# A fused attention and feed-forward kernel: the sums of probabilities times values go to any free PSUM bank instead of a fixed one, with the scheduling tables tuned anew

## The chip, the cores and the metric

One core of one Trainium2 chip. The metric is the device time of one execution in microseconds (us), as the median of several executions. A span is the time inside one profiled execution from its first to its last recorded instruction; in the profiled executions of this study it is 1.7 to 2.4 us shorter than the time. Engines are called PE (TensorE), ScalarE (ACT in the profile), VectorE (DVE), GpSimd (POOL) and SP (SyncE).

## The reference

```python
# x: 1 x 2048 x 640, bf16; H = 32 heads of Dh = 20; one K and one V head for all; F = 1536
xn = layernorm(x)
q = (xn @ wq) split into 32 heads;  k = xn @ wk;  v = xn @ wv
p = softmax(q @ k.T * Dh**-0.5)            # 32 x 2048 x 2048 probabilities
a = (p @ v) put together over heads @ wo
f = relu(xn @ w1 + b1)**2 @ w2 + b2
out = x + a + f
```

## The kernel before

The work on probabilities is cut into 2048 score tiles of 128 keys by 512 queries, each one PSUM bank. A tile's exponential is made on ScalarE (1480 tiles, two or three of them in one instruction, line 910) or approximated on VectorE and GpSimd in four terms (568 tiles). PE then adds probabilities times values ("PV") over the 16 key tiles of a block (four heads, 512 queries) in one bank, at four positions side by side. There are 32 blocks. At the end of each, VectorE copies the sum out (line 978, 30 times; the last two go another way).

The program that builds the kernel is a list scheduler: it settles the order of every engine's instructions when the kernel is built. Constants steer it, some of them in a table with an entry for each stretch of the run.

```python
NB = 7                       # banks 0..6: scores, projections, feed-forward
PVB = 7                      # bank 7: the PV sum, always
RULES = {3: {...}, 4: {...}, ...}      # steering constants by stretch  [cut]

def bank_state(bk):          # None: taken; otherwise the time from which it is free
    if bank_busy[bk]: return None
    o = bank_rel[bk]         # the instruction that empties it
    ...                                                       # [cut]

def make_act(st_):           # one exponential over n neighbouring banks
    ...
    deps = [st_["qk"]] + [pv_of[t[:2]] for t in st_["old"] if t is not None]
    return Op(..., [lambda e: e.activation(out=PT[:, s0:s0 + n, :], in_=ps[:, b0:...:db, :], func=AF.Exp, ...)], deps)

def make_pv(b, kt):          # PV of one key tile, four heads
    first, last = b not in pv_begun, pv_count[b] == KT - 1
    for h in range(HPG):
        parts.append(mm(ps[32 * h:32 * h + 32, PVB, :], vx[:, kt, :], PT[:, sl, :], first, last, (0, 32 * h)))
    if first and b > 0:
        deps.append(tn_op[b - 1])        # the copy of the block before
    ...                                                       # [cut]

# end of a block: the copy
tn = op(f"TN{b}", "DVE", 0.60, lambda e: e.tensor_copy(out=OR[:, a, :], in_=ps[:, PVB, :]), [lastpv] + or_users[a], prio=0)
```

The softmax here doesn't subtract the row's maximum and nothing guards it: scores larger than these inputs give would overflow.

## Time and profile before

The time was 705.52 us (median of 3; 704.88 to 706.26), the profiled span 703.64. The two views below were read only after the result, and they carry the explanation. The first gives the busy time of each engine by stretch of the span; the columns are the stretch, its length, then busy time and number of instructions of PE, PEld (weight loads), DVE, ACT, POOL, then clock and DMA.

```profile
0.00:40.00 40.00, 37.05 (x564) 17.29 (x565) 30.46 (x103) 31.57 (x45) 24.22 (x49) 1.00 0.48 143
40.00:694.00 654.00, 651.84 (x9062) 194.69 (x9058) 610.61 (x1013) 654.00 (x693) 401.36 (x217) 1.00 0.23 57
```

From 40 to 694 us ScalarE is busy for 654.00 of 654.00 us. The second view keeps ScalarE's groups of 45 to 694 us apart by shape; after the bar stand busy time, mean ns of one, and idle time before them.

```profile
L910 ACT ACTIVATE PT<-ps 128x1024 bf16<-128x1024 f32 x641 | 599.6, 1195 | 0.0
L910 ACT ACTIVATE PT<-ps 128x1536 bf16<-128x1536 f32 x47 | 74.6, 1617 | 0.0
```

No idle time at all. Everything before 40 us is in ScalarE's timeline (start, length, then in brackets the idle time before it):

```profile
15.30 12.46 ACT L910 ACTIVATE PT<-ps 128x1024 bf16<-128x1024 f32 x13 [1.05 <-PE ps L367]
28.15 1.94 ACT L910 ACTIVATE PT<-ps 128x1024 bf16<-128x1024 f32 x2 [0.39 <-PE ps L367]
32.44 12.88 ACT L910 ACTIVATE PT<-ps 128x1536 bf16<-128x1536 f32 x13 [2.35 <-PE ps L367]
```

After the first exponential there are two holes.

### The profile page before, as it was taken

The numbers are of one execution on the slowest core, as the hardware profiler recorded it, in microseconds if no ns is written. First come the engines' busy times: TensorE is split into PE (matmuls) and PEld (weight loads), VectorE is DVE, ScalarE is ACT, GpSimd is POOL, SyncE is SP. The second block draws the span as 40 slices with busy tenths as digits, with TensorE's granted clock in tenths as the row PEclk, the third lists the DMA queues.
The fourth block names the chain that finished last, engine by engine and source line by source line (L and its number), as shares of the span: only waits on it lengthen the run. The fifth ranks groups of instructions, "written<-read, shape, count | busy, mean of one in ns | idle before, by whom it ended". The sixth has DMA issues, their size and how long they took to land.

```text
span 703.6 us, 22608 instructions
## 1 busy us (share of the span) xinstructions
PE 695.0 (99%) x9780; PEld 216.0 (31%) x9781; DVE 645.9 (92%) x1125; ACT 687.5 (98%) x739; POOL 427.3 (61%) x268
## 2 busy tenths in 40 slices
PE   8999999999999999999999999999999999999997
PEld 4422223233322223332322222323333222233333
DVE  7789999999999998989998998899899999999894
ACT  6899999999999999999999999999999999999995
POOL 4767556567566764666568765766665675644253
PEclk9999999999999999999999999999999999999999
DMA  6325422233337701211101001111112100031201
GB/s 201 98 70 153 115 78 58 81 97 80 84 85 160 162 20 25 55 40 37 52 18 40 23 22 28 29 47 26 46 42 51 36 22 23 20 106 51 55 26 39
DMA packets 42016, 44.00 MB, mean 63 GB/s; under 512 B 15540, under 2 KB 32772, under 8 KB 41788
## 3 DMA queue, kind: packets, MB, share of 16 engines
q1 hardware_dynamic: 39132, 36.93, 19.2%
q0 software_dynamic: 2208, 5.25, 3.9%
q8 instruction: 76, 1.25, 0.7%
q10 hardware_dynamic: 576, 0.38, 0.2%
q14 instruction: 24, 0.20, 0.1%
HBM read 28.03 MB, written 14.91 MB: 61 GB/s over the span
## 4 chain that ended last, share of the span: by engine, by line
ACT 95%; PE 4%; DMA 1%; DVE 0%; SPq 0%; issue 0%; DVEq 0%
ACT PT L910 94%; PE ps L367 3%; DMA x_sb<-in_A_x_dram 1%; PE ps L540 1%; ACT xnT L477 0%; ACT OC L421 0%; DVE out_sb L1164 0%; PE ps L568 0%; SPq L384 0%; ACT OC L422 0%; SPq L391 0%; PE ps L510 0%; PE ps L496 0%; DVEq L227 0%; DVE PT L1164 0%
## 5 line engine op out<-in xcount | busy, mean ns | idle before, releaser
L910 ACT ACTIVATE PT<-ps 128x1024 bf16<-128x1024 f32 (+1 forms) x715 | 677.1, 1219 | 3.8 <-PE ps L367 3.8
L1083 DVE TENSOR_SCALAR tmore<-ps 128x512 uint16<-128x512 f32 x568 | 367.4, 683 | 31.7 <-PE ps L367 28.2
L1101 POOL TENSOR_SCALAR tmore<-tmore 128x2048 uint16<-128x2048 uint16 x109 | 206.4, 1900 | 171.1 <-PE ps L367 62.3
L367 PE MATMUL ps<-qT,kT 20*128 20x512 bf16 x2048 | 281.7, 384 | 1.9 <-ACT PT L910 0.8
L1101 POOL TENSOR_SCALAR x_sb<-tmore 128x2048 uint16<-128x2048 uint16 x100 | 189.3, 1902 | 79.4 <-DVE x_sb L1101 24.2
L367 PEld LDWEIGHTS ps<-qT,kT 20*128 20x128 bf16 x2048 | 71.6, 91 | 280.4 <-ACT PT L910 233.1
L367 PE MATMUL ps<-PT,vx 128*32 128x512 bf16 x1480 | 136.9, 386 | 0.2 <-ACT PT L910 0.2
L1101 DVE TENSOR_SCALAR x_sb<-tmore 128x2048 uint16<-128x2048 uint16 x135 | 96.1, 745 | 0.1
L367 PE MATMUL ps<-x_sb,vxs 128*32 128x512 bf16 x940 | 83.2, 382 | 0.0
L367 PE MATMUL ps<-xnT,w_sb 128*32 128x512 bf16 x960 | 77.2, 384 | 0.1
L367 PE MATMUL ps<-w_sb,big 128*32 128x320 bf16 x1536 | 74.5, 302 | 0.0
L367 PE MATMUL ps<-tmore,vxs 128*32 128x512 bf16 x764 | 69.6, 382 | 0.0
L1101 DVE TENSOR_SCALAR tmore<-tmore 128x2048 uint16<-128x2048 uint16 x82 | 61.5, 770 | 0.1
L367 PE MATMUL ps<-tmore,vx 128*32 128x512 bf16 x568 | 55.7, 382 | 0.0
L367 PEld LDWEIGHTS ps<-PT,vx 128*32 128x32 bf16 x1480 | 34.9, 94 | 62.1 <-issue 53.6
L367 PEld LDWEIGHTS ps<-w_sb,big 128*32 128x32 bf16 x1536 | 32.1, 95 | 29.3 <-issue 22.2
L648 DVE TENSOR_SCALAR hT_tmp<-ps,b1col 128x512 bf16<-128x512 f32 x48 | 35.8, 746 | 3.4 <-PE ps L367 2.7
L367 PE MATMUL ps<-xnT,wq_sb 128*32 128x512 bf16 (+1 forms) x480 | 33.7, 356 | 0.2 <-DVE tmore L1083 0.2
L367 PE MATMUL ps<-wo_c,OC 128*32 128x320 bf16 x608 | 30.9, 301 | 0.0
L367 PEld LDWEIGHTS ps<-x_sb,vxs 128*32 128x32 bf16 x940 | 21.3, 95 | 19.9 <-issue 13.4
L367 PEld LDWEIGHTS ps<-xnT,w_sb 128*32 128x32 bf16 x960 | 17.6, 94 | 26.7 <-issue 22.4
L367 PEld LDWEIGHTS ps<-tmore,vxs 128*32 128x32 bf16 x764 | 18.1, 95 | 16.4 <-issue 11.5
(81 smaller groups left out, 259.4 us busy)
## 6 DMA issues: line engine op xcount, KB each, us to landing
xbd<-b2d SPq DMA_DIRECT2D x16, 320.0 KB, 4.4
xbd<-in_A_x_dram POOLq DMA_DIRECT2D x8, 640.0 KB, 5.8
xr<-xbd SPq DMA_DIRECT2D x32, 160.0 KB, 2.4
w_sb<-in_B_w_dram SPq DMA_DIRECT2D x8, 480.0 KB, 4.4
big<-OR SPq DMA_DIRECT2D x71, 40.0 KB
big<-drs SPq DMA_DIRECT2D x71, 40.0 KB
out_dram<-out_sb SPq DMA_DIRECT2D x15, 160.0 KB, 1.8
qT<-QCr SPq DMA_DIRECT2D x108, 20.0 KB
```

The costliest lines, as they stand in the source:

```text
L367: return lambda e: e.matmul(out_, l, r, start=start, stop=stop, tile_position=tp)
L540: return [(lambda e, dt=dt: e.transpose(out=psbf(bk)[:, dt * 128:(dt + 1) * 128], in_=xn_sb[:, st, dt:D:DT], identity=ident[:])) for dt in ...
L648: o = Op(f"RL{qc}_{f}", "DVE", 0.66, [lambda e: e.tensor_scalar(out=hT_tmp[:, k % 2, :], in0=ps[:, bk, :], scalar1=b1col[:, f:f + 1], scal ...
L910: return Op(f"ACT{st_['j']}", "ACT", 0.05 + 0.4267 * n, [lambda e: e.activation(out=PT[:, s0:s0 + n, :], in_=ps[:, b0:b0 + (n - 1) * db + ...
L1083: d1 = op(f"D1_{n}_{i}", "DVE", 0.60, lambda e: e.tensor_scalar(out=L[:, cs].bitcast(U16), in0=ps[:, bank, :], scalar1=XA, scalar2=XB, op0 ...
L1101: p = op(f"P{j}_{n}", eng, 0.60 if eng == "DVE" else 1.86, lambda e, T=T, j=j, two=two: e.tensor_scalar(out=T.bitcast(U16), in0=L.bitcast( ...
```

## The change

The intent: while VectorE copies a block's sum out of the one PV bank, the next block's PV products cannot begin. If the next block may open any free bank, they need not wait.

```diff
-NB = 7
-PVB = 7
+NB = 8
+PV0 = 7
+pv_bank = {0: PV0}
+def bank_for(b):                      # the bank that is free first
+    if b in pv_bank: return pv_bank[b]
+    can = [(bank_state(bk), -bk) for bk in range(NB) if bank_state(bk) is not None and ...]
+    return -min(can)[1] if can else None
+def kept():                           # no score product takes that bank before the block has begun
+    b = pv_blk[0]
+    return bank_for(b) if b < NBLK and b not in pv_begun else None
 # make_pv, make_dpv
-        parts.append(mm(ps[32 * h:32 * h + 32, PVB, :], ...))
-    if first and b > 0:
-        deps.append(tn_op[b - 1])
+        parts.append(mm(ps[32 * h:32 * h + 32, bank, :], ...))
+    if first:
+        deps.append(bank_rel[bank])
 # the copy at a block's end
-    tn = op(..., e.tensor_copy(out=OR[:, a, :], in_=ps[:, PVB, :]), ...)
+    tn = op(..., e.tensor_copy(out=OR[:, a, :], in_=ps[:, pb, :]), ...)
+    tn.frees = pb
 # every table was tuned anew with it
-RULES = {3: {'PVA': 2.1, ...}, ...}                     # [cut]
+RULES = {2: {'ND': 1, ...}, ...}                        # [cut]
-PRIO = {'NM15': 2.12, 'NM10': 2.88, 'PW2': 0.96}
-NBEF = {'AG4': 10.21, 'NM7': 11.5, 'Qe0_1': 10.11, 'PW12': 25.33}
-QEACT = (0, 1, 2, 3)
-ACTST = (2, 5, 6)
+PRIO = {'XN1': 0.13}                                    # the start's order
+NBEF = {'S4a': 6.0, 'AG5': 10.23, 'PW1': 4.94}
+QEACT = (0, 1)
+ACTST = (0, 2, 4)
```

So the change has three parts that can be taken apart: the free bank, the table of rules, and the constants of the start. The cut parts also hold one further limit on VectorE's score products and two more constants of the start.

More of the change, by code (lines that the diff above doesn't have):

```diff
@@ L80 @@
 KEEP = 1
-RULES = {3: {'PVA': 2.1, 'PVD': 2.1, 'R3': 1, 'PP': 0.9},
-         4: {'PVA': 2.1, 'PVD': 2.1, 'R3': 1, 'PP': 0.9, 'WARM': 0.78},
-         5: {'D1P': 1, 'MPRIO': 0.5, 'PBIAS': 2.5},
-         6: {'D1P': 1, 'MPRIO': 0.5, 'PBIAS': 2.5, 'ND': 1, 'QKP': 0},
-         7: {'DQP': 2.05, 'URG': 2, 'PVD': 2.1, 'BEHIND': -0.3},
-         8: {'WARM': 0.85, 'DQP': 0.95},
-         10: {'ND': 1, 'NOPEN': 3},
-         11: {'ND': 1, 'NOPEN': 3},
-         12: {'EPS': 0.12},
-         13: {'EPS': 0.06, 'EVP': 0.3},
-         15: {'PBIAS': 0},
-         17: {'EPS': 0.06},
-         18: {'EPS': 0.12},
-         19: {'WARM': 0.78, 'PBIAS': 2.5, 'IDLE': 0.3},
-         21: {'PBIAS': 0, 'KEEP': 0},
-         23: {'EPS': 0.12},
-         25: {'R3': 1, 'EVP': 0.3},
-         26: {'R3': 1, 'EVP': 0.3, 'IDLE': 0.3, 'PVD': 2.1},
-         28: {'EPS': 0.12, 'URG': 3},
-         29: {'EPS': 0.12, 'URG': 3, 'KEEP': 3, 'EVP': 1.1, 'ND': 3},
-         31: {'PBIAS': 1, 'D1P': 1, 'PVD': 1.05},
-         32: {'PBIAS': 1, 'D1P': 1, 'PVD': 1.05, 'DGAP': 0.8, 'DQP': 0.95, 'SQP': 2, 'R3': 1},
-         36: {'PP': 0.9, 'BEHIND': -0.1, 'EVP': 0.3, 'PBIAS': 1.5},
-         37: {'URG': 3, 'JIT': 1.0, 'PVD': 1},
-         38: {'SQP': 0.7, 'URG': 3},
-         39: {'PP': 2.5},
-         40: {'PBIAS': 1},
-         41: {'PBIAS': 1, 'DGAP': 1.5, 'SQP': 0.7},
-         42: {'PBIAS': 1, 'DGAP': 1.5, 'SQP': 2, 'NOPEN': 3, 'ND': 2, 'PVD': 1},
-         43: {'PBIAS': 1, 'DGAP': 1.5, 'SQP': 2, 'NOPEN': 3, 'ND': 2, 'PVD': 1, 'R3': 9},
-         44: {'WARM': 0.78, 'KEEP': 3, 'DLAST': 7.5},
-         45: {'DGAP': 0.8, 'KEEP': 1, 'D1P': 3},
-         48: {'PBIAS': 1},
-         49: {'PBIAS': 1, 'R3': 1},
-         50: {'PBIAS': 1, 'R3': 1},
-         53: {'DLAST': 3.5},
-         54: {'DLAST': 3.5, 'EPS': 0, 'EVP': 0.3},
-         55: {'DLAST': 3.5, 'EPS': 0, 'EVP': 0.3, 'ND': 1},
-         56: {'EVP': 2, 'MPRIO': 1.0},
-         57: {'R3': 1, 'ND': 1},
-         58: {'BEHIND': -0.1, 'EPS': 0, 'PP': 4, 'R3': 1},
-         59: {'BEHIND': -0.1, 'EPS': 0, 'PP': 4, 'R3': 1, 'DRATE': 0.95, 'DLAST': 10, 'PVA': 2.1},
-         60: {'EVP': 1.1},
-         61: {'EVP': 1.1, 'SQP': 0.7},
-         62: {'EVP': 1.1, 'SQP': 0.7, 'KEEP': 3, 'R3': 1, 'NOPEN': 2, 'D1P': 3},
-         64: {'PP': 0.9, 'DRATE': 0.8},
-         65: {'R3': 1},
-         66: {'R3': 1},
-         67: {'EPS': 0.12, 'PVA': 1.05},
-         68: {'R3': 0},
-         69: {'R3': 0, 'JIT': 1.1}}
@@ new lines @@
+DJIT = 9.0
+RULES = {2: {'ND': 1, 'JIT': 1.1, 'PBIAS': 0.6},
+         3: {'DLAST': 5.5, 'NOPEN': 2, 'DJIT': 9, 'R3': 1},
+         4: {'DLAST': 5.5, 'NOPEN': 2, 'DJIT': 9, 'R3': 1, 'JIT': 0.75, 'DQP': 0.95},
+         5: {'DLAST': 5.5, 'NOPEN': 2, 'DJIT': 9, 'R3': 1, 'JIT': 0.75, 'DQP': 0.95, 'EPS': 0.12},
+         6: {'MPRIO': 0.9, 'PVD': 2.1, 'R3': 9},
+         10: {'DLAST': 7.5, 'PBIAS': 2.5, 'DGAP': 0.5},
+         11: {'DLAST': 7.5, 'PBIAS': 2.5, 'DGAP': 0.5},
+         12: {'DLAST': 5.5, 'PBIAS': 2.5, 'DGAP': 0.5, 'WARM': 0.78},
+         13: {'DLAST': 5.5, 'PBIAS': 1, 'DGAP': 0.5, 'WARM': 0.78, 'DRATE': 0.8},
+         14: {'NOPEN': 2, 'BEHIND': -0.1, 'MPRIO': 1.0},
+         15: {'IDLE': 0.5, 'NOPEN': 3, 'PVA': 1.05},
+         16: {'PP': 2.5, 'EVP': 0.5, 'PVA': 1.05, 'DGAP': 0.25},
+         17: {'DQP': 0.95, 'DJIT': 9, 'PBIAS': 1},
+         18: {'DQP': 0.95, 'DJIT': 9, 'PBIAS': 0.6, 'QKP': 0},
+         19: {'DLAST': 7.5, 'URG': 6, 'DJIT': 0.6},
+         20: {'DLAST': 6.5, 'URG': 6, 'DJIT': 0.6},
+         21: {'DLAST': 6.5, 'URG': 6, 'DJIT': 0.6, 'PVA': 1.05, 'PP': 2.5},
+         22: {'PVA': 1.05, 'JIT': 0.82},
+         23: {'PVA': 1.05, 'JIT': 0.82, 'PBIAS': 2.5, 'QKP': 0},
+         24: {'PBIAS': 2.5, 'PP': 4, 'DQP': 0.95, 'WARM': 0.72},
+         25: {'PBIAS': 2.5, 'PP': 4, 'DQP': 0.95, 'WARM': 0.72, 'MPRIO': 0.5, 'D1P': 0.5, 'DGAP': 1.5},
+         27: {'PBIAS': 2.5},
+         29: {'SQP': 2, 'URG': 2, 'PP': 2.5},
+         30: {'JIT': 0.82, 'DJIT': 0.6, 'DGAP': 1.5, 'DLAST': 2.5},
+         31: {'IDLE': 0.3, 'ND': 1, 'QKP': 0},
+         32: {'PBIAS': 0, 'JIT': 1.0},
+         33: {'JIT': 0.82, 'MPRIO': 0.9, 'PP': 2.5},
+         34: {'JIT': 0.82, 'MPRIO': 0.9, 'PP': 2.5, 'QKP': 0, 'DQP': 0.95},
+         38: {'ND': 3, 'URG': 3, 'PBIAS': 0.3, 'D1P': 0.5},
+         39: {'JIT': 0.75},
+         41: {'R3': 0},
+         42: {'SQP': 1.5, 'NOPEN': 1},
+         44: {'QKP': 0, 'R3': 1, 'BEHIND': 0.12, 'KEEP': 2},
+         45: {'QKP': 0, 'R3': 1, 'BEHIND': 0.12, 'KEEP': 3},
+         46: {'QKP': 0, 'R3': 1, 'BEHIND': 0.12, 'KEEP': 0},
+         47: {'QKP': 0, 'R3': 1, 'BEHIND': 0.12, 'KEEP': 0, 'DRATE': 1.1, 'ND': 3},
+         48: {'QKP': 0, 'R3': 1, 'BEHIND': 0.12, 'KEEP': 0, 'DRATE': 1.1, 'ND': 3},
+         49: {'QKP': 0, 'DRATE': 0.8, 'DLAST': 4.5, 'JIT': 0.75},
+         50: {'QKP': 0, 'DRATE': 0.95, 'DLAST': 4.5, 'JIT': 0.75, 'EVP': 2, 'PBIAS': 2.5},
+         51: {'QKP': 0, 'DRATE': 0.95, 'DLAST': 4.5, 'JIT': 0.75, 'EVP': 2, 'PBIAS': 2.5, 'D1P': 3, 'EPS': 0.12, 'DQP': 0.95, 'IDLE': 0.2},
+         53: {'KEEP': 3},
+         54: {'KEEP': 1, 'NOPEN': 1},
+         55: {'PP': 2.5},
+         56: {'PP': 2.5},
+         57: {'PP': 2.5, 'PVD': 0.95},
+         58: {'QKP': 0, 'URG': 6},
+         59: {'QKP': 0, 'URG': 6, 'JIT': 1.0, 'R3': 0, 'DRATE': 0.8},
+         60: {'QKP': 0, 'URG': 3, 'JIT': 1.0, 'R3': 0, 'DRATE': 0.8, 'BEHIND': 0.25, 'WARM': 0.78, 'EVP': 0.5},
+         61: {'QKP': 0, 'URG': 3, 'JIT': 1.0, 'R3': 1, 'DRATE': 0.8, 'BEHIND': 0.25, 'WARM': 0.78, 'EVP': 0.5, 'ND': 3},
+         62: {'DJIT': 0.6, 'JIT': 0.75},
+         63: {'DJIT': 0.6, 'JIT': 0.75, 'R3': 0},
+         64: {'DJIT': 0.6, 'JIT': 0.75, 'R3': 0, 'EPS': 0.06, 'PBIAS': 1.5, 'D1P': 1, 'WARM': 0.72},
+         65: {'DJIT': 0.6, 'JIT': 0.82, 'R3': 0, 'EPS': 0.06, 'PBIAS': 1.5, 'D1P': 3, 'WARM': 0.72, 'DQP': 0.95, 'SQP': 2},
+         66: {'DJIT': 9, 'JIT': 0.82, 'R3': 0, 'EPS': 0.06, 'PBIAS': 1.5, 'D1P': 3, 'WARM': 0.72, 'DQP': 0.95, 'SQP': 2},
+         67: {'DQP': 3, 'R3': 1},
+         68: {'DQP': 3, 'R3': 1, 'DGAP': 0.25, 'ND': 1, 'SQP': 2, 'PP': 4},
+         69: {'DQP': 3, 'R3': 1, 'DGAP': 0.25, 'ND': 1, 'SQP': 2, 'PP': 4}}
@@ L143 @@
 EARLYK = "F"
-FFN0 = 0.3
+FFN0 = 0.6
 OUT0 = 0.5
@@ L148 @@
 QCPOS = 0
-ACTST = (2, 5, 6)
-POOLXN = (2, 7, 9, 10, 11, 13, 14, 15)
+ACTST = (0, 2, 4)
+POOLXN = (7, 9, 10, 11, 13, 14, 15)
 ROWP = (-0.5, 0.6, 0.8, 1.2)
@@ L159 @@
 DEFAULTS = dict(EVP=EVP, PBIAS=PBIAS, MPRIO=MPRIO, DGAP=DGAP, DLAST=DLAST, DRATE=DRATE, BEHIND=BEHIND, IDLE=IDLE, URG=URG, NOPEN=NOPEN,
-                EPS=0.03, JIT=JIT, R3=R3, STATIC=STATIC, PVA=1, PVD=1, D1P=1, PP=4, SQP=2, DQP=3, QKP=0, ND=2, WARM=WARM, KEEP=KEEP)
+                EPS=0.03, JIT=JIT, R3=R3, STATIC=STATIC, PVA=1, PVD=1, D1P=1, PP=4, SQP=2, DQP=3, QKP=0, ND=2, WARM=WARM, KEEP=KEEP, DJIT=DJIT)
 class Ctr:
@@ L506, in fill_parts @@
         def fill_parts():
-            return [mm(ps[32 * jj:32 * jj + 32, PVB, :], zeros32[:, :], kT[:, 0:512], False, False, (0, 32 * jj)) for jj in range(4)]
+            return [mm(ps[32 * jj:32 * jj + 32, pv_bank[pv_blk[0]], :], zeros32[:, :], kT[:, 0:512], False, False, (0, 32 * jj)) for jj in range(4)]
         def warm_parts():
-            return [lambda e: e.matmul(ps[:, PVB, :], ones_bf[:, :], hT_tmp[:, 0, :], start=True, stop=True)]
+            return [lambda e: e.matmul(ps[:, PV0, :], ones_bf[:, :], hT_tmp[:, 0, :], start=True, stop=True)]
         def need_te(sts):
@@ L857, in make_step @@
             t0 = max(free["PE"], horizon() - par("JIT"))
-            st_of = {bk: bank_state(bk) for bk in range(NB)}
+            keep = kept()
+            st_of = {bk: bank_state(bk) if bk != keep else None for bk in range(NB)}
             ok = [bk for bk in range(NB) if st_of[bk] is not None and st_of[bk] <= t0 + 0.02]
@@ L920, in after_act, with pv_begin @@
                     pv_ready[key[0]].append(("A", key[1]))
+        pv_bank = {0: PV0}
+        bank_busy[PV0] = True
+        def bank_for(b):
+            if b in pv_bank:
+                return pv_bank[b]
+            can = [(bank_state(bk), -bk) for bk in range(NB) if bank_state(bk) is not None and not (par("STATIC") and bk in HELD)]
+            return -min(can)[1] if can else None
+        def kept():
+            b = pv_blk[0]
+            return bank_for(b) if b < NBLK and b not in pv_begun else None
+        def pv_begin(b):
+            if b not in pv_begun:
+                pv_bank[b] = bank_for(b)
+                bank_busy[pv_bank[b]] = True
+                pv_begun.add(b)
         def make_pv(b, kt):
@@ L924, in make_pv @@
             parts, deps = [], []
+            bank = bank_for(b)
             for h in range(HPG):
@@ L927, in make_pv @@
                 deps.append(o)
-                parts.append(mm(ps[32 * h:32 * h + 32, PVB, :], vx[:, kt, :], PT[:, sl, :], first, last, (0, 32 * h)))
+                parts.append(mm(ps[32 * h:32 * h + 32, bank, :], vx[:, kt, :], PT[:, sl, :], first, last, (0, 32 * h)))
             deps.append(v_op[kt // 4])
-            if first and b > 0:
-                deps.append(tn_op[b - 1])
+            if first:
+                deps.append(bank_rel[bank])
             return Op(f"PV{b}_{kt}", "PE", 0.222, parts, deps)
@@ L939, in make_dpv @@
             parts = []
+            bank = bank_for(b)
             for h in range(HPG):
                 i = s["order"].index(h)
-                parts.append(mm(ps[32 * h:32 * h + 32, PVB, :], wgt[:, kt, :], src[:, i * 512:(i + 1) * 512], first, last, (0, 32 * h)))
+                parts.append(mm(ps[32 * h:32 * h + 32, bank, :], wgt[:, kt, :], src[:, i * 512:(i + 1) * 512], first, last, (0, 32 * h)))
             deps.append(v_op[kt // 4])
@@ L945, in make_dpv @@
                 deps.append(vs_op[kt // 4][term - 1])
-            if first and b > 0:
-                deps.append(tn_op[b - 1])
+            if first:
+                deps.append(bank_rel[bank])
             return Op(f"DPV{b}_{kt}_{term}", "PE", 0.2205, parts, deps)
@@ L966, in emit_norm @@
             a = b % NOR
+            pb = pv_bank[b]
             if b >= NBLK - 2:
                 Tn, T2 = OR[:, a, :], QCr[:, 0, :]
-                tn = op(f"TN{b}", "DVE", 0.63, lambda e: e.transpose(out=Tn, in_=ps[:, PVB, :]), [lastpv] + or_users[a], prio=0)
+                tn = op(f"TN{b}", "DVE", 0.63, lambda e: e.transpose(out=Tn, in_=ps[:, pb, :]), [lastpv] + or_users[a], prio=0)
+                tn.frees = pb
                 rc = op(f"RC{b}", "DVE", 0.155, lambda e: e.reciprocal(out=Tn[:, DH:512:32], in_=Tn[:, DH:512:32]), [tn], prio=0)
@@ L977, in emit_norm @@
                 return
-            tn = op(f"TN{b}", "DVE", 0.60, lambda e: e.tensor_copy(out=OR[:, a, :], in_=ps[:, PVB, :]), [lastpv] + or_users[a], prio=0)
+            tn = op(f"TN{b}", "DVE", 0.60, lambda e: e.tensor_copy(out=OR[:, a, :], in_=ps[:, pb, :]), [lastpv] + or_users[a], prio=0)
+            tn.frees = pb
             tn_op[b] = tn
@@ L1041, in pool_banks @@
         def pool_banks():
+            keep = kept()
             if par("STATIC"):
-                return [bk for bk in POOLED if bk not in HELD and bank_state(bk) is not None]
-            fb = [bk for bk in POOLED if bank_state(bk) is not None]
+                return [bk for bk in POOLED if bk not in HELD and bk != keep and bank_state(bk) is not None]
+            fb = [bk for bk in POOLED if bk != keep and bank_state(bk) is not None]
             return fb if len(fb) > par("KEEP") else []
@@ L1055, in make_dqk @@
             if not fb or (len(fb) == 1 and behind()):
+                return None
+            if max(free["DVE"], free["PE"]) + sum(o.dur for o in dve_q if o.frees is not None) > free["PE"] + 0.43 + par("DJIT"):
                 return None
@@ L1119, in tail_bank @@
             bs = [bk for bk in range(NB) if (bk not in HELD or done) and bank_state(bk) is not None]
-            if tn_op.get(NBLK - 1) is not None and tn_op[NBLK - 1].fin is not None and not bank_busy[PVB]:
-                bank_rel[PVB] = bank_rel[PVB] or tn_op[NBLK - 1]
-                bs.append(PVB)
             return min(bs, key=lambda bk: (bank_state(bk), bk)) if bs else None
@@ L1229, in bass_parallel_sum__grouped_kv_mqa__dense_activation_squared_relu__prompt_kernel @@
             b = pv_blk[0]
-            if b < NBLK and (b == 0 or b - 1 in tn_op):
+            if b < NBLK and (b == 0 or b - 1 in tn_op) and bank_for(b) is not None:
                 for k, (kind, x) in enumerate(pv_ready[b]):
@@ L1324, in bass_parallel_sum__grouped_kv_mqa__dense_activation_squared_relu__prompt_kernel @@
             elif kind == "pv":
-                pv_begun.add(ap[1])
+                pv_begin(ap[1])
                 pv_of[(ap[1], pv_ready[ap[1]].pop(ap[2])[1])] = o
@@ L1328, in bass_parallel_sum__grouped_kv_mqa__dense_activation_squared_relu__prompt_kernel @@
             elif kind == "dpv":
-                pv_begun.add(ap[1])
+                pv_begin(ap[1])
                 s_, term = ap[3], ap[4]
```

## The prediction

> **What bounds the kernel now.** I read the page first, then the ScalarE groups kept apart by shape, the waits, the view of the line that evacuates the PV sums, and the timeline at one block's end.
>
> ```profile
> PE 695.0 (99%) x9780; PEld 216.0 (31%) x9781; DVE 645.9 (92%) x1125; ACT 687.5 (98%) x739; POOL 427.3 (61%) x268
> ...
> ACT 95%; PE 4%; DMA 1%; DVE 0%; SPq 0%; issue 0%; DVEq 0%
> ACT PT L910 94%; PE ps L367 3%; DMA x_sb<-in_A_x_dram 1%; PE ps L540 1%; ACT xnT L477 0%; ACT OC L421 0%; DVE out_sb L1164 0%; PE ps L568 0%; SPq L384 0%; ACT OC L422 0%; SPq L391 0%; PE ps L510 0%; PE ps L496 0%; DVEq L227 0%; DVE PT L1164 0%
> ```
>
> PE and ACT are both full, but a busy PE is not a PE at its peak; the chain that ended last settles it. 94% of the span lies on line 910, the exponential on ScalarE. In the chain in order of time it is one piece from 32.44 to 694.23 us.
>
> ```profile
> L910 ACT ACTIVATE PT<-ps 128x1024 bf16<-128x1024 f32 x665 | 621.9, 1190 | 1.4 <-PE ps L367 1.4
> L910 ACT ACTIVATE PT<-ps 128x1536 bf16<-128x1536 f32 x50 | 79.0, 1609 | 2.3 <-PE ps L367 2.3
> ```
>
> The work comes in 665 pairs and 50 triples of 512-column score tiles (1480 tiles; VectorE does the other 568 of 2048). Idle before them is 3.7 us in all. The mean of one (1190 ns) is longer than its turn, since neighbours overlap. From the start times of all 715 in the trace, the usual (median and 5th percentile) distance from a pair to the next start is 0.904 us; the shortest distances after a triple are 1.330 us.
>
> So the time can be taken apart:
> - first exponential starts at 15.30 us;
> - 714 full-speed turns: 664 x 0.904 + 50 x 1.330 = 666.76;
> - from first to last start there are 678.60 us, so 11.84 us are turns that came late: 3.20 before 40 us and 8.64 over the rest;
> - the last one lasts 1.25, and the tail after it 703.64 - 695.14 = 8.50;
> - time less span is 705.52 - 703.64 = 1.88.
>
> Only the start, the 8.64 and the tail can move unless tiles move between engines.
>
> Does PE wait for the evacuation of the PV sums, line 978?
>
> ```profile
> L978 DVE COPY OR<-ps x30: 674/681/692, 49.3 to 655.0; 128x512 f32<-128x512 f32 x30
> its engine sat idle before it (us, times) until:
>   PE ps L367: 0.3, 1
> who waited for it (us, times):
> busy tenths in 40 slices 0000000000000000000000000000000000000000
> ```
>
> The list under "who waited for it" is empty: no engine was seen idle for this copy. The kernel's instruction order was settled when it was built, and it puts other work there. At the block end whose copy runs from 299.99:
>
> ```profile
> 299.47 0.39 PE L367 MATMUL ps<-PT,vx 128*32 128x512 bf16 x4
> 299.83 0.39 PE L367 MATMUL ps<-qT,kT 20*128 20x512 bf16 x2
> 300.15 0.59 PE L367 MATMUL ps<-w_sb,big 128*32 128x320 bf16 x12
> ...
> 304.48 0.39 PE L367 MATMUL ps<-qT,kT 20*128 20x512 bf16 x2
> 304.80 0.40 PE L367 MATMUL ps<-PT,vx 128*32 128x512 bf16 x4
> ```
>
> PV stops at 299.86 and resumes at 304.80, with scores and feed-forward products in between and PE busy for 4.99 of the 5.00 us. Over the 30 copies the last PV of one block to the first of the next takes 1.57 to 4.94 us, median 2.2. The copy needs about 0.14 + 0.68 of that; the rest is choice of order. Nor are the late turns at those places: after 50 us they total 0.0135 us per us, and 0.014 and 0.006 us per us in the 2 us before and after a copy's start.
>
> **What the Trainium skill says.** "Perfetto Trace Analysis", section Matmuls: independent groups should rotate through PSUM banks so that evacuation of one overlaps the next group's products. That is the intent here, but the trace shows the overlap already had by other means. The same page, section Optimization Strategy, says that repeating bubbles on the engine that should be full can mean too little buffer. Here they are small: 480 of the 691 turns after 40 us are within 5 ns of the fastest, and the largest delay is under 0.3 us. "ScalarE: Activation LUTs", section "Step-by-step: what each stage is for", gives 0.833 ns per element whatever the function. The trace agrees: (1.330 - 0.904) / 512 = 0.832 ns. So the turns themselves cannot shrink.
>
> **The change part by part.**
> 1. The bank. The fixed PV bank goes; scores, projections and PV draw from eight. While a block is summing, seven are left, as before. At a block end the next PV may open another bank, so the pause can fall from a median of 2.2 us toward nothing. But while the next block has not begun, the best free bank is kept back for it, so scores gain little. What this saves in PE idle is zero by the view above. It lets the order be better balanced; of 8.64 us of late turns I give it 1, an estimate.
> 2. The split of work. Built, both programs have 2048 score products, 568 VectorE tiles, 3752 PV products and the same feed-forward products. ScalarE gets 657 pairs, 55 triples, 1 single: still 1480 tiles. Turns: 657 x 0.904 + 55 x 1.330 = 667.08, and the last single lasts about 1.19 - 0.43 = 0.76, together 667.84 against 666.76 + 1.25 = 668.01. Worth 0.2 us.
> 3. VectorE and GpSimd. Of the passes that derive further terms, 11 move to GpSimd (217 to 206 on DVE, 209 to 220 on POOL). That frees 11 x about 0.75 = 8 us of a VectorE that is 92% busy and not the bound, and adds 11 x 1.9 = 21 to a GpSimd at 61%. Neither is on the chain. PE gets 5 more warm-up products and 4 more zero products, under 3 us of filler in its waits.
> 4. The start, retuned along with it. ScalarE takes the statistics of row tiles 0, 2, 4 in place of 2, 5, 6 and hands two query evacuations (0.28 each) to VectorE; the order of normalizing and transposing changes. Two effects:
>    - First exponential. Now VectorE does statistics of a later tile from 7.88 and normalizes an early one only at 9.96; in the new order the early tiles come sooner. I estimate 0.5 to 1.5 us earlier, say 1.0.
>    - Third group of keys. The first 32 score tiles need only the first two groups, then ScalarE stands still, 30.09 to 32.44, for the third: VectorE copies two query evacuations (0.69 each, at 25.15 and 27.10) and only then normalizes a tile at 28.16 that the group needs. In the new order only one such copy lies ahead, and the second projection's 20 products (about 1.1 us of PE) come after the group. This could take most of the 2.35 us away, but an earlier first exponential also makes it ask earlier. For the 3.20 us of late turns I put 1.7.
>
>    Together about 2.5 us.
> 5. The tail. The last products are interleaved otherwise: after the final transpose 64 output products remain in place of 56. 8 x 0.034 us (16 took 0.54) is 0.3 worse; the shorter last exponential has been counted.
>
> Sum: -1.0 (late turns) - 0.2 (turns) - 2.5 (start) + 0.3 (tail) = -3.4 us, so 705.5 - 3.4 = 702.1; I say 702.
>
> **The rivals.**
> - Nothing comes of it: PV was never seen waiting, ScalarE's tiles are unchanged, and the start only shifts its waiting from one place to another. 705, plus or minus 1. For it speak the empty list and the keys gate; against it the 2.35 us hole with two avoidable copies ahead of it.
> - The late turns vanish: the 8.64 us come from PE being tied, and free banks loosen it. Best case 705.5 - 8.6 - 3.2 - 1.5 = 692, 1.9% faster, so not even this passes 2%. Against it: late turns do not gather at block ends.
> - A new wait: a score product meets a bank that VectorE has not emptied, or a GpSimd pass (1.9 us against 0.75) arrives late for its PV because 11 more were handed there. VectorE's busy share speaks for the first, GpSimd's 61% against the second. Doubling the late turns costs about 8 us: 711 at worst with a gain at the start.
>
> **Range and chances.** Spread comes from the start (-4 to +1) and the late turns (-4 to +3), not independent of how well the order suits the chip: 698 to 706. Past 2% needs under 691.4 or over 719.6; the first needs more than all the waste listed, the second more than twice today's late turns. Chances: faster 0.03, within 2% 0.95, slower 0.02.
>
> **What would show it.** Pair and triple turns should stay 0.904 and 1.330; late turns after 40 us should be 6 to 10 us; the hole near 32 us should be under 1.5; the first exponential should lie between 13.5 and 15.3; the tail should be 8.3 to 9.2; the pause between blocks' PV should shrink with PE no busier. I am wrong if the pause shrinks and the late turns fall to a third (the bank was what tied PE), or if they grow (the order no longer fits the chip).

## The result and the profile after

The changed kernel is correct and takes 706.59 us (median of 4; 706.53 to 707.07), against 705.81 (704.88 to 706.26) for the kernel before, timed with it. The ratio is 1.0014, 95% interval 0.9997 to 1.0032: the same. Here and below a ratio is the mean time of one kernel's fast runs over that of the other's fast runs of the same rounds, so not quite the ratio of the medians quoted. All runs were fast, except one of pin_new, which is left out.

The page after: the busy times, then the chain that ended last by engine.

```profile
PE 695.3 (99%) x9790; PEld 217.7 (31%) x9790; DVE 643.3 (91%) x1117; ACT 687.8 (98%) x735; POOL 446.5 (63%) x278
...
ACT 61%; PE 37%; DVE 1%; DMA 1%; issue 0%; POOL 0%; ACTq 0%; DVEq 0%
```

VectorE lost 2.6 us of work and GpSimd gained 19; PE and ScalarE stand as before. The chain now runs through PE for 37% of the span, where it had been 4%. That looks like a new bound and is not one. The chain is followed back from the end and steps onto PE where an exponential had to wait for it, then stays there: from such a wait at 639.53 us it runs back on PE to 444.17. One real wait, however small, sends it there for a long way. ScalarE's groups from 45 to 694 us, and the stretches, say how small:

```profile
L918 ACT ACTIVATE PT<-ps 128x1024 bf16<-128x1024 f32 x636 | 595.1, 1187 | 0.6 <-PE ps L374 0.3
L918 ACT ACTIVATE PT<-ps 128x1536 bf16<-128x1536 f32 x49 | 78.1, 1614 | 0.0
```

```profile
40.00:694.00 654.00, 651.70 (x9065) 195.66 (x9057) 609.86 (x1006) 653.42 (x690) 422.39 (x230) 1.00 0.23 57
```

ScalarE is idle for 0.6 us in 654. The pause that the change was made for did go: from the end of the last PV product of one block to the start of the first of the next it was 2.2 us (median of 30 blocks; mean 2.77), and is now 0.03 us in the mean and 0.49 at most. In 17 of the 30 blocks there is none at all: the first product starts before the modelled end of the last. PE got no less idle by it: from 40 to 694 us it is busy for 651.84 us before and 651.70 after. The pause had been full of other products all along.

**The start.** ScalarE's timeline after the change:

```profile
14.88 7.44 ACT L918 ACTIVATE PT<-ps 128x1024 bf16<-128x1024 f32 x8 [1.97 <-PE ps L374]
23.22 7.13 ACT L918 ACTIVATE PT<-ps 128x1024 bf16<-128x1024 f32 x6 [0.91 <-PE ps L374]
31.01 7.74 ACT L918 ACTIVATE PT<-ps 128x1536 bf16<-128x1536 f32 x7 [0.66 <-PE ps L374]
39.73 6.03 ACT L918 ACTIVATE PT<-ps 128x1536 bf16<-128x1536 f32 x6 [0.98 <-PE ps L374]
```

The hole of 2.35 us near 32 us has become three holes of 0.91, 0.66 and 0.98. Each ends 0.6 to 1.1 us after the keys of another group of four key tiles have been written by VectorE, and it begins where ScalarE had used up the groups that it had: 16 score tiles (of 16 per group) were done before the first, and 31 and 47 before the others, whose exponentials cover three tiles and so reach into the next group. Here are those writes, groups two, three and four, first before and then after the change:

```profile
19.35 0.75 DVE L554 TENSOR_SCALAR kT<-ps,nk 128x512 bf16<-128x512 f32 x1
30.94 0.75 DVE L554 TENSOR_SCALAR kT<-ps,nk 128x512 bf16<-128x512 f32 x1 [1.58 <-PE ps L367]
35.13 0.75 DVE L554 TENSOR_SCALAR kT<-ps,nk 128x512 bf16<-128x512 f32 x1 [1.80 <-PE ps L367]
```

```profile
21.36 0.75 DVE L561 TENSOR_SCALAR kT<-ps,nk 128x512 bf16<-128x512 f32 x1
29.67 0.75 DVE L561 TENSOR_SCALAR kT<-ps,nk 128x512 bf16<-128x512 f32 x1
38.16 0.75 DVE L561 TENSOR_SCALAR kT<-ps,nk 128x512 bf16<-128x512 f32 x1 [1.80 <-PE ps L374]
```

The third group comes 1.27 us sooner, the second 2.0 and the fourth 3.0 us later.

**Reading ScalarE by its ends.** The prediction took the span apart by the starts of the exponentials. Taken apart by their ends, the picture is another. In the kernel before, the distance from one end to the end of the next pair is 0.915 to 0.919 us from the 1st to the 99th percentile of the pairs after 40 us (the longest is 0.919 too, so not one pair ended late), and 1.342 to 1.345 for a triple: 0.833 ns per column plus 0.063 us per instruction. The starts lie 0.904 us apart most of the time, so they run ahead by 0.013 us per turn, until one is held back by its score product and the lead is used up. In the table, the column after the first end is the sum of 714 such end-to-end distances at full rate, a gap is what a distance has over that, and the tail is what follows the last exponential's end.

| kernel | first exponential ends | 714 distances at full rate | gaps before 40 us | gaps after 40 us | tail | span |
|---|---|---|---|---|---|---|
| before | 16.32 | 675.86 | 2.96 | 0.00 | 8.50 | 703.64 |
| after (712 distances) | 15.90 | 675.73 | 3.47 | 0.92 | 8.78 | 704.80 |
| difference | -0.42 | -0.13 | +0.51 | +0.92 | +0.28 | +1.16 |

After 40 us the kernel before had nothing left to lose or to win on ScalarE. The changed kernel has 0.92 us of gaps, 0.90 of it in three places: at 445.58, 473.61 and 639.53 us. Here is the last; the idle time of a weight load stands beside what the profile names as its releaser.

```profile
637.02 0.40 PE L374 MATMUL ps<-qT,kT 20*128 20x512 bf16 x4
...
637.63 0.89 PE L374 MATMUL ps<-PT,vx 128*32 128x512 bf16 x12
...
638.07 0.69 DVE L1011 COPY OR<-ps 128x512 f32<-128x512 f32 x1 [0.35 <-PE ps L374]
...
638.56 0.60 PE L374 MATMUL ps<-x_sb,vxs 128*32 128x512 bf16 x8
...
639.09 0.09 PEld L374 LDWEIGHTS ps<-qT,kT 20*128 20x128 bf16 x2 [0.42 <-DVE OR L1011]
639.10 0.39 PE L374 MATMUL ps<-qT,kT 20*128 20x512 bf16 x2
...
639.53 2.37 ACT L918 ACTIVATE PT<-ps 128x1024 bf16<-128x1024 f32 x2 [0.34 <-PE ps L374]
```

Two groups of score products start 2.08 us apart (637.02 and 639.10), with other products between them, and the exponential came late. The profile puts the score product's wait down to the copy of the PV sum, line 1011. Whether that is so is a question for an experiment (a_quarter below).

### The profile page after: what moved, and what is told of

Its sections match the earlier page's. It is cut to its first block, busy times and chain, and to the rows that moved or that the text cites. A ratio compares the mean times of both kernels' runs of the same rounds, so it can differ in the third digit from the quotient of the medians.

```text
span 704.8 us, 22625 instructions
## 1 busy us (share of the span) xinstructions
PE 695.3 (99%) x9790; PEld 217.7 (31%) x9790; DVE 643.3 (91%) x1117; ACT 687.8 (98%) x735; POOL 446.5 (63%) x278
## 4 chain that ended last, share of the span: by engine, by line
ACT 61%; PE 37%; DVE 1%; DMA 1%; issue 0%; POOL 0%; ACTq 0%; DVEq 0%
ACT PT L918 61%; PE ps L374 35%; DMA x_sb<-in_A_x_dram 1%; PE ps L547 0%; PE ps L575 0%; PE ps L517 0%; DVE out_sb L1198 0%; PE ps L482 0%; DVE xnT L550 0%; PE ps L503 0%; POOL rstd L441 0%; DVE OR L433 0%; DVE big L443 0%; DVE OR L434 0%; ACTq L391 0%
## 5 line engine op out<-in xcount | busy, mean ns | idle before, releaser
L1138 POOL TENSOR_SCALAR tmore<-tmore 128x2048 uint16<-128x2048 uint16 x114 | 215.8, 1903 | 113.5 <-DVE tmore L1138 38.1
L1138 POOL TENSOR_SCALAR x_sb<-tmore 128x2048 uint16<-128x2048 uint16 x106 | 200.5, 1899 | 116.5 <-PE ps L374 40.9
L1138 DVE TENSOR_SCALAR x_sb<-tmore 128x2048 uint16<-128x2048 uint16 x129 | 93.9, 752 | 0.1
L374 PE MATMUL ps<-xnT,w_sb 128*32 128x512 bf16 x960 | 75.5, 383 | 0.0
```

Of the source, the lines that this page charges most:

```text
L374: return lambda e: e.matmul(out_, l, r, start=start, stop=stop, tile_position=tp)
L1138: p = op(f"P{j}_{n}", eng, 0.60 if eng == "DVE" else 1.86, lambda e, T=T, j=j, two=two: e.tensor_scalar(out=T.bitcast(U16), in0=L.bitcast( ...
```

## The experiments

**The theories at the beginning.** A: the wait for the evacuation was hidden before and is worth nothing; ScalarE's 1480 tiles fix the time; the late starts that I had counted (8.6 us after 40 us) come from score products queued behind other PE work. B: the free bank is a gain of its own, hidden because the tables are worth more. C: ScalarE alone sets the time, and PE's work does not bear on it. D: PE sets the time (b_lightpe takes 12 to 17 us off, b_light2 no more than 17). "Frozen order" means that only what an instruction does is changed, when it is written out, so the order of all engines stays that of the kernel named.

### b_quarter: the copy of the PV sum made short

```diff
-    lambda e: e.tensor_copy(out=OR[:, a, :], in_=ps[:, PVB, :])
+    lambda e, w=512 if b < NOR else 128: e.tensor_copy(out=OR[:, a, 0:w], in_=ps[:, PVB, 0:w])
```

> Kernel before, same order of all instructions, but from the fourth block on the evacuation of the PV sums (line 978) copies 128 of the 512 columns (wrong result on purpose), so that each bank comes free about 0.4 us sooner and VectorE has about 27 x 0.4 = 11 us less to do. Theory A (the wait for the evacuation was hidden before the change): 705 to 706.5 us, late exponential turns after 40 us stay at 8.6 plus or minus 1. Rival B (the wait cost time, and the change gave it back elsewhere): 700 to 703 us, late turns below 6.

Measured: 705.55 us, ratio 0.9997 (0.9982 to 1.0012); gaps after 40 us by ends -0.03, which is nil. Twenty-seven of the copies were truly short (forms and durations of the copy's line):

```profile
L978 DVE COPY OR<-ps x30: 275/281/684, 49.4 to 655.1; 128x128 f32<-128x128 f32 x27, 128x512 f32<-128x512 f32 x3
```

A copy shorter by 0.4 us, 27 times, gives nothing. The evacuation itself was not on the path.

### b_lightpe: less feed-forward work on PE

```diff
+    if o.name.startswith(("OUT", "FP")) and o.name.split(".")[1] in ("4", "5", "6", "7"):
+        o.parts = []        # 4 of the 12 products of each half of an output tile are left out
```

> Kernel before, same order, with 4 of the 12 second feed-forward products of each of 32 output halves left out (wrong result on purpose): 128 groups of 0.136 us, 17 us less PE work, ScalarE untouched. Theory A (ScalarE is full and PE is within some 3% of full, so PE's order makes exponential turns late): time falls by 2 to 5 us, late turns after 40 us from 8.6 to 4 to 6.5. Rival C (ScalarE alone sets the time): within 1 us of before. Rival D (PE sets the time): falls by 12 to 17 us.

Measured: 706.03 us, ratio 1.0005 (0.9989 to 1.002). PE's busy time fell from 695.0 to 680.0 us and nothing came of it. Theory A's 2 to 5 us were wrong, and so were D's 12 to 17; C's "within 1 us" holds.

### b_lightact and b_light2: less work on ScalarE, alone and with b_lightpe

```diff
-    e.activation(out=PT[:, s0:s0 + n, :], in_=ps[:, b0:...:db, :], ...)
+    w = 512 if step < 24 else 480
+    e.activation(out=PT[:, s0:s0 + n, 0:w], in_=ps[:, b0:...:db, 0:w], ...)
```

> Kernel before, same order, each exponential from the 25th turn on covering 480 of the 512 columns of a tile (wrong result on purpose): about 1430 tiles x 0.0266 us = 38 us less ScalarE work, PE untouched. Theory A: PE, which had some 20 us idle between 40 and 694 us, takes over: time falls by 10 to 20 us, the exponentials wait for score products in most turns. Rival C (ScalarE alone): falls by 33 to 38 us.

> Both lightenings together (wrong result on purpose). Theory A: the gains add up, since each engine had been held by the other: falls by 22 to 34 us. Rival C: same as the exponential's lightening alone, 33 to 38 us. Rival D: no more than 17 us.

Measured: 696.72 us, ratio 0.9876 (0.9857 to 0.9895) with ScalarE alone lighter; 690.03 us, ratio 0.9775 (0.9758 to 0.9791) with both. By ends: 38.1 us of ScalarE's work went, and 29.1 us of true gaps came in the first, 22.9 in the second. So PE does limit the kernel as soon as ScalarE is faster, some 9 us below today's time, and then PE's own work counts. C, right for b_lightpe, falls with b_lightact. A's direction holds, but its sizes were too large: 9.2 us came off in place of 10 to 20, and 15.9 in place of 22 to 34. That is within D's 17, but D itself had fallen with b_lightpe.

### b_lightpv and b_pvall: shorter PV products, in a few places and everywhere

```diff
-    parts.append(mm(ps[32 * h:32 * h + 32, PVB, :], wgt[:, kt, :], src[:, i * 512:(i + 1) * 512], first, last, ...))
+    w = 256 if term == 3 and not first and not last else 512      # b_lightpv
+    w = 512 if first or last else 384                              # b_pvall, in make_pv too
+    parts.append(mm(ps[32 * h:32 * h + 32, PVB, 0:w], wgt[:, kt, :], src[:, i * 512:i * 512 + w], first, last, ...))
```

> Kernel before, same order, with the fourth PV product group of each VectorE set (term 3, 142 of them, where it neither opens nor closes a sum) cut to 256 of 512 columns (wrong result on purpose): about 15 us less PE work, as in the lightened feed-forward run, but taken from the PV products. In the trace of before all 86 late turns over 0.02 us had a score product queued directly behind other PE products, mostly these, with its bank free for at least 0.2 us. Theory A' (late turns come from PV products packed ahead of score products): late turns after 40 us from 8.6 to 3 to 5.5, time 3 to 5.5 us less. Rival C (ScalarE alone, PE's order does not matter): within 1 us, late turns 8.6.

> The kernel before in its own frozen order, with nearly every PV product (all terms, except the one that opens and the one that closes a block's sum) cut from 512 to 384 columns. The result is wrong on purpose; the order and the number of instructions are unchanged. Some 870 groups of four times a quarter of about 0.21 us, an estimate of 46 us less PE work, spread evenly over the whole run instead of in a few places as in the two light-PE runs before. Theory E1 (the late turns are local: score products queued behind other PE products at places that the earlier cuts did not reach): the late turns after 40 us fall from 8.6 to under 3 us and the time falls by 5 to 8 us (697 to 700.5). Theory E2 (late turns come from the order itself, from waits for ScalarE's own banks, and not from how long PE's products last): the late turns stay at 7 to 9 us and the time stays within 1.5 us of the kernel before.

Measured: b_lightpv 705.74 us, ratio 0.9997 (0.9972 to 1.0023); b_pvall 705.50 us, ratio 1.0000 (0.9983 to 1.0017). PE's busy time was 690.0 and 671.0 us, which is 5 and 24 us less than before, where about 15 and 46 had been expected. The late starts stayed at 8.87 and 8.49 us. Single ones shrank (one of 0.178 us to 0.069 in b_lightpv), others took their place. A sum that 24 us less busy PE does not touch cannot be made of PE's work. E2's numbers hold, but its reason, waits for ScalarE's own banks, was wrong as well. The view that gave it away is ScalarE's groups in b_pvall from 45 to 694 us:

```profile
L910 ACT ACTIVATE PT<-ps 128x1024 bf16<-128x1024 f32 x641 | 603.1, 1269 | 0.0
L910 ACT ACTIVATE PT<-ps 128x1536 bf16<-128x1536 f32 x47 | 78.1, 1706 | 0.0
```

With PE lighter, the mean exponential got longer, 1269 ns in place of 1195, over the same 1024 columns, at the same pace. A recorded exponential is work plus the time for which it stood behind the one before. One that found ScalarE idle lasts 1.02 us (the first: 15.30 to 16.32). What it has above that is how early it was fed. PE's gain went there: score products came earlier and waited longer.

### b_act508 and b_act500: ScalarE's rate, one for one

The same edit as b_lightact with 508 and 500 in place of 480 columns. If the late starts were no loss, then ScalarE's rate fills the stretch, and every bit of its work that goes must come off the time in full, until PE is met.

> The kernel before in its own frozen order, each exponential from the 25th turn on over 508 instead of 512 columns of a tile (the other four columns keep an old value; wrong on purpose). Read by the ENDS of the exponentials, the kernel before has no late turn at all after 40 us: each pair ends 0.917 us after the one before, each triple 1.343 us, which is 0.833 ns per column and 0.063 us per instruction. Theory R (ScalarE's own rate fills the whole stretch, the 8.64 us of late starts are no loss): 1429 shortened tiles times 4 columns times 0.833 ns = 4.8 us less, one for one, and the gaps by ends stay under 0.6 us: 700.7 to 701.5, ratio 0.9925 to 0.994. Rival W (the late starts are real waits for score products): the shorter work is swallowed by them, and less than half, 0 to 2.4 us, comes off.

> As the run with 508 columns, with 500: the work of ScalarE falls by 1429 times 12 times 0.833 ns = 14.3 us. With 480 columns 38.1 us of work went and 29.1 us of real gaps came, 9.0 left. Theory R: ScalarE first gains one for one, then PE takes over; expected 5 to 8 us of gaps by ends, so 6 to 9 us less than the kernel before, 696.5 to 699.5. Rival W: 0 to 5 us less.

Measured: b_act508 700.81 us, ratio 0.9928 (0.9915 to 0.994), 4.9 us less than the kernel before in the same rounds, for 4.8 us less work; gaps after 40 us 0.01. b_act500 697.21 us, ratio 0.9879 (0.9864 to 0.9894), 8.5 us less for 14.3 us less work; gaps after 40 us 5.6. (Both leave columns out: measuring tools, not better kernels.) The rival W is out. In b_act500 the groups of 45 to 694 us and the chain show where PE takes over:

```profile
L910 ACT ACTIVATE PT<-ps 128x1000 bf16<-128x1000 f32 x641 | 584.9, 1037 | 0.2
```

```profile
PE 93%; ACT 4%; DVE 1%; DMA 1%; SPq 0%; issue 0%; DVEq 0%
```

The mean of 1037 ns is close to the shortest in that stretch (998): exponentials are no longer fed early. The idle column still says 0.2 us, though 5.6 us of gaps are there by ends: an exponential that starts a little before the one ahead has ended hides the gap.

### pin_none and free_none: the free bank without tables

Both with the old constants of the start and an empty table; pin_none is the kernel before, free_none the kernel after with them. (pin_none was made from the code after, with the bank rule undone. It and the kernel before with an empty table give the same instructions.)

```diff
-RULES = {...}
+RULES = {}
```

> Fixed PV bank, the old start settings, but the table of ordering rules by stage emptied. Theory A (the tables are what the time hangs on, and each fits one kernel): 8 to 16 us slower than before, 714 to 722. Rival B (the fixed bank costs time by itself): much slower than the same with a free bank, by 4 us or more.

> Free PV bank, the old start settings, no table of rules: differs from the fixed-bank run without a table in the bank rule alone. Theory A: within 5 us of it, in either direction, 714 to 724. Rival B: at least 4 us faster than it.

Measured: 715.12 us, ratio 1.013 (1.0104 to 1.0156), and 720.17 us, ratio 1.0201 (1.0171 to 1.0231). The free bank alone is 5 us slower here. Both give ScalarE 1488 tiles. Gaps after 40 us are 2.30 with the pinned bank and 1.46 with the free one, and tails 11.33 and 16.66: the loss lies wholly in how the end falls. B, in which the free bank gains 4 us or more, falls; A's "within 5 us" is met but for 0.05. The 0.84 us of gaps is the only trace of a gain.

### pin_new: the tables made for the free bank, on a pinned one

```diff
-NB = 8
+NB = 7
 def bank_for(b):
-    ...
-    return -min(can)[1] if can else None
+    return PV0 if bank_state(PV0) is not None else None
```

> The changed kernel with the bank rule undone (PV pinned to bank 7, scores on the other seven), with its new table and start settings. Theory A: the table does not fit this bank rule, 713 to 720, so 6 to 13 us slower than the changed kernel, and no less than the old table costs the free bank. Rival E (the new table is worth as much by itself): 703 to 708.

Measured: 717.70 us (median of three runs; the fourth, slow, took 729.84), ratio 1.0168 (1.0136 to 1.02), 11.1 us over the changed kernel. By parts of the profiled execution (718.75 us, the slowest of the three) against it: 9.1 us more work at full rate (ScalarE gets 1500 tiles in place of 1480), 2.8 us more gaps, 0.4 more tail. This does not make the free bank worth 11.1 us. The table steers a scheduler that now takes other decisions; it fits the one order that it was made for. The counterpart, the old table on a free bank, was not run, so the last clause of theory A stays open.

### pin_newstart and free_oldstart: only the start's constants exchanged

```diff
-PRIO = {'NM15': 2.12, 'NM10': 2.88, 'PW2': 0.96}; QEACT = (0, 1, 2, 3); ACTST = (2, 5, 6); ...
+PRIO = {'XN1': 0.13};                             QEACT = (0, 1);       ACTST = (0, 2, 4); ...   # pin_newstart; the reverse in free_oldstart
```

> The kernel before (pinned bank, its own table of block rules) with only the start's constants of the kernel after. The start by itself: first exponential plus late turns before 40 us is 15.30 + 3.20 = 18.50 us in before and 14.88 + 3.76 = 18.64 in after. Theory S1 (the start's holes are only moved by the new start order): the first exponential at 14.8 to 15.0 and the sum of both at 18.2 to 19.0. Theory S2 (the start order by itself does gain the 2.5 us that I predicted, and the freed bank or the new block rules take it away): the sum is 15.5 to 16.8. For the whole: since the table of block rules was fitted to the old start, the time is 708 to 716 in either case.

> The kernel after (any free bank, its own table of block rules) with only the start's constants of the kernel before. Theory S1 (the start order only moves the holes): first exponential 15.2 to 15.5, first exponential plus late turns before 40 us 18.2 to 19.0 us. Theory S2 (the new start order gains 2 us or more, hidden by other losses): the sum is 20.5 or more. For the whole: the block rules were fitted to the new start, so 709 to 717 us in either case; if it is within 1.5 us of after (706.6), the tables do not depend on the start as I believe.

Measured: 719.78 us, ratio 1.0202 (1.0186 to 1.0217), and 720.64 us, ratio 1.0215 (1.02 to 1.0231): both slower than I had expected, since the tables no longer fit (ScalarE gets 1500 tiles in both). By starts, the first exponential plus late turns before 40 us came to 17.71 and 19.21 us, between S1 and S2 in the first and just over S1's range in the second (where the first exponential, at 15.04, lay below S1's 15.2). By ends, the first end plus the gaps before 40 us is 19.28 in before, 18.49 in pin_newstart, 19.37 in after and 19.96 in free_oldstart. So up to 40 us the new start is worth 0.6 to 0.8 us where it alone is exchanged, and nothing in the pair itself. Even that is hardly beyond doubt: in the nine runs with before's own order the same sum lies between 18.76 and 19.37, and pin_newstart has a further gap of 0.93 us at 43.45, just after the line drawn at 40; with it the sum is 19.42. S2's 2 to 3 us are excluded. The key groups follow the constants and not the bank: in pin_newstart their writes start at 21.28, 29.62 and 37.74, as after the change; in free_oldstart at 19.09, 31.57 and 36.49, as before it.

### a_quarter: the short copy in the changed kernel

The edit of b_quarter, in the changed kernel.

> The kernel after in its own order, with the copy of each PV sum cut from 512 to 128 columns from the fourth block on (wrong result on purpose). In the kernel before the same edit gave nothing (0.9997). Theory N (the freed bank made a new wait: at a block's end two banks are held until the copy is through, and three late turns of 0.31 to 0.69 us come from that): late turns after 40 us fall from 9.5 to 8.0 to 8.8 us, the three large ones shrink below 0.3 each, and the time falls by 0.5 to 1.5 us. Rival (the extra lateness of after is only how its order falls and has nothing to do with the copy): late turns 9.2 to 9.8 us, the large ones unchanged, time within 0.4 us of after.

Measured: 706.67 us, ratio to the kernel before 1.0015 (1.0 to 1.003), as the changed kernel; gaps after 40 us 0.91, with the three large ones unchanged (0.23, 0.23, 0.44 in both). Theory N falls. The same place in this run:

```profile
638.03 0.29 DVE L1011 COPY OR<-ps 128x128 f32<-128x128 f32 x1 [0.34 <-PE ps L374]
...
639.05 0.39 PE L374 MATMUL ps<-qT,kT 20*128 20x512 bf16 x2
639.05 0.09 PEld L374 LDWEIGHTS ps<-qT,kT 20*128 20x128 bf16 x2 [0.42 <-DVE out_sb L739]
```

The copy is over 0.7 us before the score product starts, the score product starts just as late, with the same 0.42 us before its weights, and the profile now names another instruction. The named releaser was only the last semaphore that it needed; what held the score product was the products ahead of it in PE's queue. Over the whole run, the list of who waited for the copy shrinks from 2.1 us in 5 waits to 0.8 us in 2, and the time stays:

```profile
L1011 DVE COPY OR<-ps x30: 675/681/693, 50.4 to 658.0; 128x512 f32<-128x512 f32 x30
...
  PEld ps L374: 2.1, 5
```

```profile
L1011 DVE COPY OR<-ps x30: 275/280/691, 50.4 to 658.0; 128x128 f32<-128x128 f32 x27, 128x512 f32<-128x512 f32 x3
...
  PEld ps L374: 0.8, 2
```

One gap of the three, that at 445.58, does begin with something new: at 444.17 PE waited 0.19 us to open block 20's sum, for a bank that ScalarE was emptying, and four PV groups stood ahead of the score product. In the gap at 639.53 too, products of a block that has just opened (block 29, from 637.90) stand ahead of the score product. Products that can start at once, where the fixed bank had kept them back, may thus be what delays the score products in two of the three places; that these gaps would be gone with a fixed bank was not tried by itself.

## Why the prediction was right or wrong

The prediction said 702.0 us, 698 to 706, and the same within 2%. It is 706.59, so the class was right and the time lies 0.6 us outside the range. The recorded sum was -3.4 us; in the span it is +1.16 (one profiled execution each, and the times do not differ beyond noise). Step by step:

**Right: the wait for the evacuation was hidden.** The empty list behind the copy and the block end with PE busy said so, and b_quarter (0.9997) and a_quarter (unchanged) showed it. The pause shrank from 2.2 us to next to nothing and PE got no busier, as I had written.

**Right: the turns (-0.2; measured -0.13) and the tail (+0.3; measured +0.28).** The split of tiles and the count of closing products could be taken from the built program, and the durations from the trace.

**Right in direction, of no weight: VectorE and GpSimd.** I had counted 8 us less on the first and 21 more on the second; it is 2.6 less and 19 more, and neither bounds anything.

**Wrong, by 2.6 us: the start, "Together about 2.5 us".** It measured -0.42 + 0.51 = +0.09. Half of the reasoning held: the third group's keys came 1.27 us sooner, and the hole near 32 us fell from 2.35 to 0.66. But I followed the one group at which ScalarE stood still before, and not the groups beside it. The new order takes the work of the second (2.0 us later) and the fourth (3.0 us later) to pay for it, and ScalarE stands still there instead. The rival "nothing comes of it" had named this: the start only shifts its waiting. Nor was the first exponential's 1.0 us to be had: it measured 0.42. That is not even beyond doubt, since nine runs with before's own order (before and the frozen ones) put the first exponential's end between 15.80 and 16.41 us, and the four with the new start between 15.71 and 15.90.

**Wrong in kind: the 8.64 us of "turns that came late", of which I took 1.** They were no loss. By ends, not one exponential after 40 us of the kernel before came late (gaps 0.00). The sum is bookkeeping: 691 turns times the 0.0127 us by which the usual start-to-start distance (0.904) is shorter than the end-to-end distance (0.917) is 8.8 us. Four runs with lighter PE or a shorter copy left it at 8.5 to 8.9, and b_act508 took 4.9 us off the time for 4.8 us of ScalarE's work, which a stretch with 8.6 us of waits in it could not have done. The contradiction lay in my own text: I quoted 3.7 us of idle time for this line and counted 11.84 us of lateness. The rival "the late turns vanish", with its best case of 692, could not exist for the same reason, and it pulled the range downward. The Trainium skill, "Perfetto Trace Analysis", section Identifying the Most-Contended Engine, holds occupancy to be a fair measure for ScalarE but not PE's busy share; the trace agrees on both: 654.00 of 654.00 us on ScalarE, and a PE at 99% that gave up 24 us unnoticed.

**What came instead: 0.92 us of true gaps**, in three places where PE's queue has about 1 to 2 us of other products ahead of a score product. It is no wait for the copy (a_quarter). By PE's order in the trace it is how the new order happens to fall; whether the free bank or the tables made it fall so was not tried.

So the expected gain did not go anywhere, for it never existed: the kernel before was at ScalarE's rate from 34 us to 695. What could still be won without taking work from ScalarE was the start and the tail. PE is 5 to 9 us behind as the next limit (b_act500, b_lightact). The tables matter more than the bank: without its table the pinned kernel loses 9.8 us (715.12 against 705.32 in the same rounds). No version beats both kernels with a full computation.

## What to carry to other kernels

Before giving a price to "late" instructions on a busy engine, read the same stretch by their ends: if the ends are evenly spaced, the engine is full, a longer record means only that the instruction was fed earlier, and no better order helps. A wait that an in-order queue has already filled with other work is worth nothing when it is removed; shorten what is waited for and measure before building the change. When one hole in a start-up is closed, ask which neighbour's work was put off for it.

## What the Trainium skill lacked or had wrong

- "Perfetto Trace Analysis", section Per-instruction lifecycle: it puts the recorded start of a ScalarE instruction at the moment when it begins executing and has left the queue. In the kernel before, equal exponentials whose ends are 0.917 us apart are recorded as 1.06 to 1.33 us long, and one that found the engine idle as 1.02. Here a start can lie up to 0.3 us ahead of that, and starts drift ahead by 0.013 us per turn. The page does not say for ScalarE that rates are to be read from ends.
- "Perfetto Trace Analysis", section Matmuls: it advises rotating banks so that evacuation overlaps the next group's products. With an order fixed at build that filled the pause with other products, the rotation took the pause from 2.2 us (median) to 0.03 (mean) and left the time as it was (ratio 1.0014, 0.9997 to 1.0032). The page does not name the case.
- "ScalarE: Activation LUTs", section What ACT_TABLE_LOAD costs: 186 ns plus 0.833 ns per column alone, and about 93 ns of overlap back to back. Measured here for an exponential from PSUM: 1.02 us alone at 1024 columns (the page's figures give 1.04) and 0.917 in a row (they give 0.946). The slope agrees, but the constant in a row is 0.063 us and not 0.093; over 714 exponentials the difference comes to an estimated 21 us.
- No page that I read says that the releaser which a trace names for an instruction behind a full queue may not be what held it: here the same 0.42 us was put down to the copy in one run and to another instruction in the next (a_quarter).
